# Flat weight loads of 4.5 rows per partition, one transfer for wo, w2 in halves, and 128 of its rows in three row pieces

## The chip, the cores and the metric

One core of a Trainium2 chip. The time is the device time of one execution in microseconds (us); each kernel is run several times, always beside runs of the kernel before on the same chip. "The record" of a transfer is its entry in the trace: queue, start, duration and size of each packet. The records of a load to 128 partitions are 128 packets and 16 semaphore writes, so I count 8 packets for each of the 16 DMA engines. A semaphore write is the packet by which an engine reports that its part of a load is done; the last of the 16 is the load's landing. The records do not say which engine a packet ran on.

## The reference

A decode step: attention over a window of 2,048 cached positions, and a squared-ReLU MLP beside it, for two tokens.

```python
# B, Sq, D = 2, 1, 576;  Hq, Hkv, Sk, Dh = 32, 16, 8192, 128;  F = 4608;  all bf16
xn = layernorm(x)
q  = (xn @ wq)                               # wq: 576 x 4096
k, v = last 2048 positions of the caches     # 2 x 16 x 2048 x 128 each
o  = softmax(q k^T * Dh**-0.5) v
h  = relu(xn @ w1 + b1) ** 2                 # w1: 576 x 4608
out = x + o @ wo + h @ w2 + b2               # wo: 4096 x 576, w2: 4608 x 576
```

The weights and the window are 53.6 MB. Each byte is used once per call.

## The kernel before

K and V come in sixteen loads of 2 MB, 16,384 B per partition. A weight with 576 rows is 4 rows per partition plus a remainder of 64 rows. wo comes in two transfers, w2 in four row groups, whose last is itself cut. 256 rows of w2 do not fit that scheme: they come by small loads on the scalar queue, w2x, four of 5 partitions x 8 rows each and one of 96 partitions x 1 row.

```python
XS = ((8, 20, 5), (1, 96, 96))               # (rows per partition, partitions, partitions per load)
# ... cut ...
def issue_w2x():
    if x_parts:
        s, i = x_parts.pop(0)
        xr, xp, xe = XS[s]
        rows = B_w2[FX[s]:FX[s] + xr * xp, :].rearrange("(e i r) n -> i e (r n)", e=xe, r=xr)
        tc.keep_in_program_order(nc.scalar.dma_start(out=w2x_sb[s][i:xp:xp // xe, :], in_=rows[i]))
# ... cut: issue_w2x is called behind K and V loads, one small load each ...
W2P = [(0, 0, 9), (1, 0, 9), (2, 0, 9), (3, 0, 4), (3, 4, 6), (3, 6, 7)]     # (group, first row, last row)
# ... cut: the loop over eight units of K and V ...
for u in range(2, NU):
    step(u)
    # ... cut: load_v, load_k ...
    if u == 4:
        issue_wo(0)
        for i in range(NW):
            issue_w1(i)
wo_sel(0); wo_acc(0); issue_wo(1)
for w in W2P:
    issue_w2(*w)
```

Of the kernel before, what the change touches and what calls it, by code (L numbers as in the profile page):

```python
# [16 lines left out]
def kernel(  # L17
# [38 lines left out]
    SR = NS * NC  # L56
    assert SR == 32 and NG % NT == 0

    NFULL = D // P
    REM = D - NFULL * P  # L60
    S = P // REM
    KC = NFULL + 1
    NXN = NFULL + S
    LQ = (Hq * Dh) // S
    L1 = F // S
    NG4 = 4
    QW = Hq * Dh // NG4
    QB = QW // 2
    QH = QW // Dh
    HW = F // NG4  # L70
    HB = HW // 3
    FR = HW // P
    XS = ((8, 20, 5), (1, 96, 96))
    FT = (HW - sum(r * p for r, p, _ in XS)) // P
    F3 = (NG4 - 1) * HW
    CX = [(r, FT, P) for r in range(FT)]
    FX = []
    for xr, xp, _ in XS:
        FX.append(F3 + FT * P + sum(m * n for m, n, _ in XS[:len(FX)]))
        CX += [(FX[-1] - F3 + r, xr, xp) for r in range(xr)]  # L80
    assert FX[-1] + XS[-1][0] * XS[-1][1] == F
    N3 = (NG4 - 1) * FR
    NFC = N3 + len(CX)
    RB = 32 * (NG4 - 1) + B
# [4 lines left out]
    NP = NQ // 2  # L89
    WR = 2 * NC * Dh // P  # L90
    assert Dh // WR == NC
# [3 lines left out]
    kvpool = ctx.enter_context(tc.tile_pool(name="kvpool", bufs=6))  # L95
    ktpool = ctx.enter_context(tc.tile_pool(name="ktpool", bufs=2))
    wbig = ctx.enter_context(tc.tile_pool(name="wbig", bufs=1))
    wrem = ctx.enter_context(tc.tile_pool(name="wrem", bufs=1))
    wopool = ctx.enter_context(tc.tile_pool(name="wopool", bufs=1))
# [11 lines left out]
    out2d = out.rearrange("b s d -> (b s) d")  # L111

    k_tiles, v_tiles, wq_tiles, w1_tiles, wo_tiles, w2_tiles = {}, {}, {}, {}, {}, {}
    WBW = max(Hq * Dh, F)
    WRW = max(LQ, L1)

    def unit_view(cache, u):
        tq, b = divmod(u, B)
        return cache[b, tq * TH:(tq + 1) * TH, S0:Sk, :].rearrange("h (c j) d -> c h (j d)", c=CP)

    def issue_kv(tiles, cache, u, name, parts=1):
        tl = kvpool.tile([P, UE], BF16, tag="kv", name=f"{name}_{u}")
        v = unit_view(cache, u)
        n = UE // parts
        tiles[u] = tl
        return [lambda i=i: nc.sync.dma_start(out=tl[:, i * n:(i + 1) * n], in_=v[:, :, i * n:(i + 1) * n])
                for i in range(parts)]

    def issue_w(tiles, wt, i, name, width, lrem):
        if i == 1:  # L130
            tl = wbig.tile([P, NFULL * WBW], BF16, tag="wbig", name=f"{name}_big")
            nc.sync.dma_start(out=tl[:, 0:NFULL * width],
                              in_=wt[0:NFULL * P, :].rearrange("(p r) n -> p (r n)", r=NFULL))
            for r in range(NFULL):
                tiles[r] = tl[:, r * width:(r + 1) * width]
        else:
            tl = wrem.tile([P, WRW], BF16, tag="wrem", name=f"{name}_rem")
            nc.sync.dma_start(out=tl[:, 0:lrem], in_=wt[NFULL * P:D, :].rearrange("r (s l) -> (r s) l", s=S))
            tiles[NFULL] = tl

    def issue_wq(c):
        issue_w(wq_tiles, A_wq, c, "wq", Hq * Dh, LQ)

    def issue_w1(c):
        issue_w(w1_tiles, B_w1, c, "w1", F, L1)

    def w_rows(tiles, c, col0, n, L):
        if c < NFULL:
            return tiles[c][:, col0:col0 + n], c
        sg = col0 // L  # L150
        assert (col0 + n - 1) // L == sg
        return tiles[c][:, col0 - sg * L:col0 - sg * L + n], NFULL + sg

    def issue_wo(t):
        tl = wopool.tile([P, WR, D], BF16, tag="wo_sb", name=f"wo_{t}")
        n = P * WR
        nc.sync.dma_start(out=tl[:], in_=A_wo[t * n:(t + 1) * n, :].rearrange("(p r) n -> p r n", r=WR))
        wo_tiles[t] = tl

    w2_last = []  # L160

    def issue_w2(g, r0, r1):
        nr = FR if g < NG4 - 1 else FT
        if g < NG4 - 1:
            tl = kvpool.tile([P, nr * D], BF16, tag="kv", name=f"w2_{g}")[:]
        else:
            if r0 == 0:
                w2_last.append(wbig.tile([P, nr * D], BF16, tag="wbig", name=f"w2_{g}"))
            tl = w2_last[0][:, r0 * D:r1 * D]
        rows = B_w2[g * HW:g * HW + nr * P, :].rearrange("(p r) n -> p (r n)", r=nr)  # L170
        nc.sync.dma_start(out=tl, in_=rows[:, r0 * D:r1 * D])
        w2_tiles[(g, r0)] = tl

    const.tile([P, 96], F32, name="pad_0")
    w2x_sb = [const.tile([xp, xr * D], BF16, name=f"w2x_sb_{i}") for i, (xr, xp, _) in enumerate(XS)]
    const.tile([P, 120], F32, name="pad_1")
    x_parts = [(s, i) for s, (_, xp, xe) in enumerate(XS) for i in range(xp // xe)]

    def issue_w2x():
        if x_parts:  # L180
            s, i = x_parts.pop(0)
            xr, xp, xe = XS[s]
            rows = B_w2[FX[s]:FX[s] + xr * xp, :].rearrange("(e i r) n -> i e (r n)", e=xe, r=xr)
            tc.keep_in_program_order(nc.scalar.dma_start(out=w2x_sb[s][i:xp:xp // xe, :], in_=rows[i]))

# [7 lines left out]
    for f in issue_kv(k_tiles, A_k_cache, 0, "k"):  # L193
        f()
    NW = 2
    for i in range(NW):
        issue_wq(i)
    tmp_f = work.tile([P, NS, Dh], F32, tag="o_sb", name="tmp_f")
# [21 lines left out]
    for i in range(2):  # L220
# [7 lines left out]
    tmp_x = work.tile([P, NS, Dh], F32, tag="o_sb", name="tmp_x")  # L228
    tmp_xb = tmp_x[:].bitcast(BF16).rearrange("p s d -> p (s d)")
    xn_sb = tmp_xb[0:B, 0:D]  # L230
    nc.vector.tensor_scalar(out=xn_sb, in0=x_sb, scalar1=mv[:, 0:1], scalar2=rstd[:, 0:1],
                            op0=ALU.subtract, op1=ALU.mult)
    xr_sb = tmp_xb[0:B, D:D + S * P].rearrange("p (s k) -> p s k", s=S)
    nc.vector.memset(xr_sb, 0.0)
    for sg in range(S):
        nc.vector.tensor_copy(out=xr_sb[:, sg, sg::S], in_=xn_sb[:, NFULL * P:D])

    pro_ps = psum.tile([P, NXN, B], BF16, tag="o", name="pro_ps")
    for c in range(NFULL):
        transpose(out=pro_ps[:, c, :], in_=xn_sb[:, c:NFULL * P:NFULL], identity=ident[:B, :B])  # L240
    for sg in range(S):
        transpose(out=pro_ps[:, NFULL + sg, :], in_=xr_sb[:, sg, :], identity=ident[:B, :B])
    xnT = const.tile([P, NXN, B], BF16, name="xnT")
    nc.vector.tensor_copy(out=xnT[:], in_=pro_ps[:])

    own = const.tile([P, NC], F32, name="own")
    nc.vector.tensor_reduce(out=own[:], in_=ident[:].rearrange("p (a c) -> p c a", c=NC), axis=AX.X, op=ALU.add)
    off = const.tile([P, NC], F32, name="off")
    nc.vector.tensor_scalar(out=off[:], in0=own[:], scalar1=BIG, scalar2=-BIG, op0=ALU.mult, op1=ALU.add)
    HQ = P // 2  # L250
    of_h = const.tile([P, 3 * HQ], F32, name="of_h")
    nc.gpsimd.memset(of_h[:], 0.0)
    nc.vector.tensor_copy(out=of_h[:, HQ:2 * HQ].rearrange("p (c q) -> p c q", c=NC),
                          in_=own[:].unsqueeze(2).to_broadcast([P, NC, HQ // NC]))
# [7 lines left out]
    is_h = ident[0:TH, 0:TH].unsqueeze(1).to_broadcast([TH, NJJ * 32 // TH, TH])  # L262
    out_ps = psum.tile([RM, OQ], F32, tag="out", name="out_ps")
    nc.vector.memset(out_ps[:], 0.0)

    def out_acc(lhsT, rhs_of, start=False, stop=False):
        for i in range(4):
            matmul(out_ps[32 * i:32 * i + MB, :], lhsT=lhsT, rhs=rhs_of(i * OQ, (i + 1) * OQ), start=start, stop=stop,
                   skip_group_check=True, tile_position=(0, 32 * i))

    QZ = 2 * NC
    qz = const.tile([P, NQ, B, 2, 3 * QZ], BF16, name="qz")
    nc.gpsimd.memset(qz[:], 0.0)
    q_ps = []
    for k in range(2):
        q_ps.append(psum.tile([P, QB], F32, tag=("o", "op")[k], name=f"q_ps_{k}"))
        nc.vector.memset(q_ps[k][:], 0.0)

    def q_block(c):
        for k in range(2):  # L280
            for g in range(NG4):
                rhs, xc = w_rows(wq_tiles, c, g * QW + k * QB, QB, LQ)
                matmul(q_ps[k][32 * g:32 * g + B, :], lhsT=xnT[:, xc, :], rhs=rhs,
                                 start=(c == 0), stop=(c == KC - 1), skip_group_check=True,
                                 tile_position=(0, 32 * g))
        if c == KC - 1:
            qrow = const.tile([RB, 2 * QW], BF16, tag="row", name="qrow")
            for k in range(2):
                cp = nc.scalar.copy if k else nc.vector.tensor_copy
# [268 lines left out]
    for w in W2P:  # L558
        issue_w2(*w)
# [45 lines left out]
```

## Time and profile before

| | before |
|---|---|
| time, median of 3 runs | 134.31 us (134.27 to 134.45) |
| span in the profile | 132.6 us |
| packets on the main DMA queue (q1) | 4,032 |
| packets on the scalar queue (q10) | 178 |
| last landing (last semaphore write on q1) | 129.12 us |
| last landing to end of the span | 3.5 us |

The lines that the prediction reads are shown in it. Two more views matter later. The first is the windows view (columns: stretch, length, busy time and count of PE, PEld, DVE, ACT, POOL, granted clock, DMA share, GB/s):

```profile
19.00:30.00 11.00, 8.65 (x73) 4.06 (x73) 2.73 (x7) 2.00 (x6) 0.36 (x1) 0.66 1.01 430
50.00:61.00 11.00, 8.54 (x84) 5.05 (x82) 7.02 (x17) 5.46 (x7) 0.36 (x1) 1.00 1.00 424
```

The share says how long the engines were busy, the rate what they moved. The first stretch has a full share (1.01) at 430 GB/s; the second is full too (1.00) at 424, and it is the stretch in which the kernel's 96-row load is under way (issued at 47.2 us). The second view is the DMA issues (KB, and us to landing where known) of w2's small loads:

```profile
w2x_sb<-in_B_w_dram ACTq DMA_DIRECT2D x4, 45.0 KB
w2x_sb<-in_B_w_dram ACTq DMA_DIRECT2D x1, 108.0 KB, 8.5
```

### The profile page before, as it was taken

What the parts mean: (1) busy time and instruction counts of PE and PEld (TensorE: products, weight loads), DVE (VectorE), ACT (ScalarE), POOL (GpSimd) and SP (SyncE); (2) the same over time, 40 slices, a digit from 0 to 9 for tenths busy, and PEclk for the clock granted to TensorE, in tenths of its full rate; (3) what the DMA queues carried; (4) which work ended last, traced back from release to release, by engine and by line L of the source; (5) the groups of instructions that cost most, each with busy time, mean ns of one, the idle gap of its engine ahead of it and who ended that gap; (6) DMA issues with size and microseconds to landing.
All of it is one profiled execution on the core that took longest, in us unless ns stands there. A gap on an engine that the chain in (4) does not pass through costs nothing.

```text
span 132.6 us, 2337 instructions
## 1 busy us (share of the span) xinstructions
PE 84.1 (63%) x982; PEld 52.2 (39%) x982; DVE 57.2 (43%) x156; ACT 46.7 (35%) x64; POOL 5.2 (4%) x17
## 2 busy tenths in 40 slices
PE   0069409599597669298496599697500938655941
PEld 0068303257364436164254346354300424414930
DVE  6724400525477456566377446575400043344000
ACT  5715500418874375176265255194200040000000
POOL 6000000010010010100100100100100000000000
PEclk9999955958999999999999769999985595555595
DMA  4999999999999999999999999999999999999960
GB/s 139 409 415 488 425 397 416 430 430 415 444 418 431 433 420 427 431 430 430 418 440 420 440 430 432 421 457 432 478 405 388 425 425 450 407 423 428 416 247 1
DMA packets 4219, 53.76 MB, mean 405 GB/s; under 512 B 503, under 2 KB 730, under 8 KB 1246
## 3 DMA queue, kind: packets, MB, share of 16 engines
q1 hardware_dynamic: 4032, 53.32, 94.6%
q10 hardware_dynamic: 178, 0.31, 0.6%
q8 instruction: 7, 0.11, 0.3%
q14 instruction: 2, 0.02, 0.0%
HBM read 53.62 MB, written 0.00 MB: 404 GB/s over the span
## 4 chain that ended last, share of the span: by engine, by line
DMA 62%; PE 4%; DVE 1%; ACT 1%; issue 1%; ACTq 0%
DMA v<-in_A_v_cache_dram 29%; DMA w<-in_B_w_dram 17%; DMA k<-in_A_k_cache_dram 16%; PE kT_ps L108 3%; PE o_ps L105 1%; ACT kT L325 1%; PE sc_ps L105 1%; ACT p L357 1%; DVE pT L360 1%; DVE kT L327 0%; DVE o L386 0%; PE out_ps L105 0%; ACT fin_sb L573 0%; DVE o L384 0%; PE op_ps L105 0%
## 5 line engine op out<-in xcount | busy, mean ns | idle before, releaser
L108 PE MATMUL kT_ps<-ident_f,k 128*128 128x128 f32 x256 | 40.0, 303 | 9.3 <-DMA k<-in_A_k_cache_dram 7.0
L108 PEld LDWEIGHTS kT_ps<-ident_f,k 128*128 128x128 f32 x256 | 31.5, 155 | 22.6 <-issue 11.6
L325 ACT COPY kT<-kT_ps 128x1024 bf16<-128x1024 bf16 x32 | 32.0, 1012 | 21.8 <-PE kT_ps L108 17.4
L327 DVE COPY kT<-kT_ps 128x1024 bf16<-128x1024 bf16 x32 | 21.8, 682 | 12.9 <-PE kT_ps L108 12.7
L105 PE MATMUL sc_ps<-kT,qz 128*32 128x512 bf16 x128 | 10.3, 403 | 6.4 <-DVE kT L327 5.0
L357 ACT ACTIVATE p<-sc_ps,bias 128x512 bf16<-128x512 f32 x8 | 5.5, 688 | 17.6 <-DVE gown L353 17.6
L105 PE MATMUL o_ps<-v,pT 128*32 128x512 bf16 x128 | 11.6, 461 | 0.0
L105 PEld LDWEIGHTS <-xnT 128*2 128x2 bf16 x100 | 3.1, 112 | 17.7 <-issue 17.5
L105 PE MATMUL h_ps<-w_big,xnT 128*2 128x384 bf16 x48 | 3.6, 484 | 7.9 <-DMA w_big<-in_B_w_dram 7.9
L346 DVE TENSOR_REDUCE m<-sc_ps 128x1 f32<-128x512 f32 x8 | 5.5, 692 | 7.1 <-PE sc_ps L105 7.1
L386 DVE SCALAR_TENSOR_TENSOR o<-o_ps,in_s,o 128x128 f32<-128x128 f32 x24 | 8.3, 348 | 0.5
L360 DVE STREAM_TRANSPOSE pT<-p 128x512 bf16<-128x512 bf16 x8 | 5.7, 711 | 6.5 <-ACT p L357 6.5
L573 ACT CAST fin_sb<-out_ps 113x144 bf16<-113x144 f32 x1 | 0.3, 279 | 21.8 <-PE out_ps L105 21.8
L105 PE MATMUL q_ps<-wq_big,xnT 128*2 128x512 bf16 x32 | 3.6, 625 | 5.0 <-DMA wq_big<-in_A_wq_dram 5.0
L350 POOL PARTITION_ALL_REDUCE gmax<-m x8 | 2.9, 365 | 88.8 <-DVE m L348 88.8
L384 DVE TENSOR_SCALAR o<-o_ps,in_s 128x128 f32<-128x128 f32 x8 | 2.7, 341 | 8.1 <-PE o_ps L105 8.1
L451 DVE TENSOR_TENSOR hrow<-t 98x384 bf16<-98x384 f32 x3 | 1.6, 557 | 10.6 <-ACT t L450 10.5
L105 PEld LDWEIGHTS <-qz 128*32 128x32 bf16 x128 | 2.2, 96 | 10.1 <-DVE kT L327 7.5
L105 PE MATMUL op_ps<-o,of_h 128*128 128x129 f32 x16 | 3.9, 333 | 3.2 <-DVE o L386 3.2
L105 PEld LDWEIGHTS <-hT_sb 128*17 128x17 bf16 (+2 forms) x172 | 4.3, 116 | 3.2 <-issue 3.2
L105 PE MATMUL out_ps<-w,hT_sb 128*17 128x144 bf16 x136 | 4.1, 279 | 2.1 <-DMA w<-in_B_w_dram 2.0
L450 ACT ACTIVATE t<-h_ps 98x384 f32<-98x384 f32 x3 | 1.4, 489 | 11.0 <-PE h_ps L105 10.7
(74 smaller groups left out, 52.8 us busy)
## 6 DMA issues: line engine op xcount, KB each, us to landing
k<-in_A_k_cache_dram SPq DMA_DIRECT2D x8, 2048.0 KB, 18.3
v<-in_A_v_cache_dram SPq DMA_DIRECT2D x8, 2048.0 KB, 9.9
wo<-in_A_wo_dram SPq DMA_DIRECT2D x2, 2304.0 KB, 27.2
w_big<-in_B_w_dram SPq DMA_DIRECT2D x1, 4608.0 KB
wq_big<-in_A_wq_dram SPq DMA_DIRECT2D x1, 4096.0 KB, 17.8
w<-in_B_w_dram SPq DMA_DIRECT2D x3, 1296.0 KB, 31.6
w_rem<-in_B_w_dram SPq DMA_DIRECT2D x1, 576.0 KB, 28.0
w<-in_B_w_dram SPq DMA_DIRECT2D x1, 576.0 KB, 22.1
```

The costliest lines, as they stand in the source:

```text
L105: tc.keep_in_program_order(nc.tensor.matmul(*a, **k))
L108: tc.keep_in_program_order(nc.tensor.transpose(*a, **k))
L325: nc.scalar.copy(out=kT, in_=kT_ps[:])
L327: nc.vector.tensor_copy(out=kT, in_=kT_ps[:])
L346: nc.vector.tensor_reduce(out=m1[:], in_=sc_ps[:], axis=AX.X, op=ALU.max)
L350: nc.gpsimd.partition_all_reduce(gmax[:], m2[:], channels=P, reduce_op=ReduceOp.max)
L357: nc.scalar.activation(out=p_sb[:], in_=sc_ps[:], func=ACT.Exp, bias=bias[:, 0:1], scale=scale, accum_out=o1[:, Dh:Dh + 1])
L360: nc.vector.transpose(out=pT[:].rearrange("p j r -> p (j r)"), in_=p_sb[:])
L384: nc.vector.tensor_scalar(scalar1=in_s[:, 0:1], scalar2=None, op0=ALU.mult, **kw)
L386: nc.vector.scalar_tensor_tensor(scalar=in_s[:, k:k + 1], in1=o1[:, 0:Dh], op0=ALU.mult, op1=ALU.add, **kw)
L450: nc.scalar.activation(out=t1, in_=mlp["ps"][k][0:RB, :], func=ACT.Relu)
L451: nc.vector.tensor_tensor(out=hrow[:, k * HB:(k + 1) * HB], in0=t1, in1=t1, op=ALU.mult)
```

## The change

The intent is fewer and larger packets, and small loads that are spread better over the DMA engines. wq, w1 and wo are each read flat, in one transfer, with 4.5 rows per partition. A row that straddles two partitions is handled by a stationary tile (the operand that TensorE holds while the weights stream past it) of four columns, two tokens x two halves. wo moves to the end. w2 is two halves of 18 rows per partition: the first half is one transfer, the second comes as rows 0 to 8, 9 to 13, 14 to 15 and 16 on the main queue. Its row 17, one row of 1,152 B for each of 128 partitions, is the new w2x, cut into partitions 0 to 84, 85 to 116 and 117 to 127. The change was also described as bringing K and V in 16 KB packets; that was already so. The core of the diff, cut:

```diff
-    NFULL = D // P
-    REM = D - NFULL * P
-    XS = ((8, 20, 5), (1, 96, 96))
+    W2P = [(0, 9), (9, 14), (14, 16), (16, 17)]
+    XS = [(0, 85), (85, 117), (117, 128)]
 ...
+    def issue_flat(w, name):
+        n = w.shape[0] * w.shape[1] // P
+        tl = wbig.tile([P, NH * L1], BF16, tag="wbig", name=name)
+        nc.sync.dma_start(out=tl[:, 0:n], in_=w.rearrange("r n -> (r n)").rearrange("(p l) -> p l", p=P))
+        return tl
 ...
+    for p0, p1 in XS:
+        nc.scalar.dma_start(out=w2x_sb[p0:p1, :], in_=w2_rows[1, p0:p1, (FR - 1) * D:FR * D])
     step(1)
     load_k(4)
 ...
-    wo_sel(0)
-    wo_acc(0)
-    issue_wo(1)
-    for w in W2P:
-        issue_w2(*w)
+    mlp_h(w1_sb)
+    wo_sb = issue_flat(A_wo, "wo")
 ...
+    nc.sync.dma_start(out=w2a_sb[:], in_=w2_rows[0])
+    nc.sync.dma_start(out=w2b_sb[:], in_=w2_rows[1, :, 0:r9 * D])
+    for r0, r1 in W2P[1:]:
+        nc.sync.dma_start(out=w2c_sb[:, (r0 - r9) * D:(r1 - r9) * D], in_=w2_rows[1, :, r0 * D:r1 * D])
```

## The prediction

> **What bounds the kernel now.** I read the page's 40 slices and packet counts first, because the reference reads every weight and cache byte once and does little arithmetic with it:
>
> ```profile
> PE   0069409599597669298496599697500938655941
> ...
> DMA  4999999999999999999999999999999999999960
> ...
> DMA packets 4219, 53.76 MB, mean 405 GB/s; under 512 B 503, under 2 KB 730, under 8 KB 1246
> ...
> q1 hardware_dynamic: 4032, 53.32, 94.6%
> q10 hardware_dynamic: 178, 0.31, 0.6%
> ```
>
> The DMA row is at 9 from the second slice to the last but two, while PE has holes. The reader is to see that no engine waits for long because of its own work: 94.6% + 0.6% of 132.6 us is 126.2 us of packets on each of 16 DMA engines, in a span that holds about 127 us between the first packet and the last. Next, the windows view at the two ends (columns: stretch, length, busy time and count of each engine, clock, DMA share, GB/s):
>
> ```profile
> 22.00:42.00 20.00, 16.22 (x143) 9.53 (x135) 10.56 (x26) 11.18 (x17) 0.73 (x2) 0.87 1.01 429
> ...
> 62.00:82.00 20.00, 14.72 (x132) 8.74 (x130) 12.28 (x30) 9.29 (x12) 0.73 (x2) 0.91 1.01 431
> ...
> 126.00:127.00 1.00, 0.00 (x0) 0.00 (x0) 0.00 (x0) 0.00 (x0) 0.00 (x0) 0.94 0.99 393
> 127.00:128.00 1.00, 0.74 (x36) 0.59 (x36) 0.00 (x0) 0.00 (x0) 0.00 (x0) 1.00 0.73 280
> 128.00:129.00 1.00, 0.43 (x16) 0.28 (x16) 0.00 (x0) 0.00 (x0) 0.00 (x0) 1.00 0.41 144
> 129.00:130.00 1.00, 0.59 (x12) 0.24 (x11) 0.00 (x0) 0.20 (x1) 0.00 (x0) 0.77 0.01 2
> ```
>
> In the middle the share is 1.01 at 427 to 431 GB/s: full. At the end it falls to 0.73 and 0.41 while the last bytes come: some DMA engines are done at 127.0 and others at 129.1. If all finished together they would finish about (1 - 0.73) + (1 - 0.41) + 0.1 = 0.96 us earlier. That is the only idle DMA time after the start. Third, the chain in order of time, and the timeline at the end:
>
> ```profile
> 68.31 39.02 DMA v<-in_A_v_cache_dram
> 107.33 0.02 issue
> 107.34 22.09 DMA w<-in_B_w_dram
> ```
>
> ```profile
> 128.39 0.43 PE L105 MATMUL out_ps<-w,hT_sb 128*17 128x144 bf16 x16 [0.65 <-DMA w<-in_B_w_dram]
> 129.10 0.66 PE L105 MATMUL out_ps<-w,hT_sb 128*17 128x144 bf16 x12 [0.28 <-DMA w<-in_B_w_dram]
> 129.80 0.28 ACT L573 CAST fin_sb<-out_ps 113x144 bf16<-113x144 f32 x1 [21.76 <-PE out_ps L105]
> 130.11 0.63 ACTq L574 DMA_DIRECT2D out_dram<-fin_sb  x1
> ```
>
> The chain's long pieces are issue-to-landing times in a full queue, so they are queueing, not latency. After the last byte (129.1) come four matmuls, a cast and the store: 132.6 - 129.1 = 3.5 us.
>
> **What the Trainium skill says.** "DMA: Bandwidth & Descriptors", Where 436 GB/s comes from, puts the ceiling at 435 GB/s; the 427 to 431 of the windows agree: no room in the rate. The same page, Why small descriptors are slow, names a fixed overhead per packet. The trace's packet records agree that one exists: packets of 1,152, 16,384 and 36,864 B take 51, 611 and 1,364 ns (medians), a line of 36.7 ns per 1,000 B plus 9 ns. The same page, Why a DMA increments its semaphore by 16 and not by 1, says a load uses the largest number of engines up to 16 that divides its slowest dimension, the lowest-numbered ones. The records agree in the count: each 5-partition w2x load left 5 semaphore writes and the 2-partition load of x left 2. By that, the 85-partition piece of the change goes to 5 engines, the 32-partition piece to 16, the 11-partition piece to 11.
>
> **The change part by part.** Bytes: the five tensors and both caches are read once before and after, 53.6 MB. K and V were 16 KB packets already (2,048 packets of 16,384 B in the records), so that part of the description moves nothing.
>
> *Packets, the main queue.* Per DMA engine a 128-partition load has 8 packets. Before, outside K and V: 4,096 + 32,768 (wq), 4,608 + 36,864 (w1), 2 x 18,432 (wo), 3 x 10,368, 4,608, 2,304, 1,152 (w2): 159 + 1,213 + 178 + 1,364 + 2 x 686 + 3 x 389 + 178 + 93 + 51 = 5,775 ns, x 8 = 46.20 us. After: wq and wo 36,864 each, w1 41,472 (1,364 + 4,608 x 0.0367 = 1,533), w2 20,736 (771), 10,368 (389), 5,760 (220), 2,304 (93), 1,152 (51): 5,785 ns, x 8 = 46.28 us. One more row of w2 per partition comes through here, for 12 loads turned into 8. With four semaphore writes of 9 ns fewer per engine: +0.04 us.
>
> *Packets, the scalar queue.* w2x before: four loads of 5 x 9,216 B (347 ns) and 96 rows of 51 ns. Engines 0 to 4 carry 4 x 347 + 6 x 51 = 1.69 us, the others 0.31. After, 128 rows of 51 ns: engines 0 to 4 carry 17 + 2 + 1 = 20 rows, 1.02 us; the others 2 or 3, 0.10 to 0.15. Engine 0 also carried four b1 packets of 93 ns; it now has two of about 51. So with the +0.04: engines 0 to 4 gain 0.6 us, engine 0 about 0.9, the others 0.1 to 0.2. The mean gain is some 0.29 us, which is about 31 packets fewer per engine at 9 ns.
>
> *Which engine ends last.* The last load's 16 semaphore writes in the records stand from 128.24 to 129.12, with 128.86 next to last. One engine trails by about 0.3 from 50 us on, when the 2,304 B packets of b1 have gone by; I take it for engine 0. The ones behind it can be those that served the seven 16 KB instruction fetches (queue 8; each pushes one engine back by roughly 1 us). Engine 0 comes forward by 0.9, to 128.2; the fetch engines by only 0.13, from 128.86 to 128.7. The end of the stream then moves from 129.12 to about 128.7: 0.4 us. That the fetches fall as before is assumed.
>
> *TensorE.* The q product goes from 40 matmuls of 512 columns to 36; the stationary tile has four columns for two, and a moving column costs the same. h goes from 60 of 384 to 72 of 288: at 2.40 us for 32 in the timeline at half clock (75 ns each), 4.5 us becomes 72 x 75 x 0.75 = 4.1. Output products: 64 + 64 for wo as before, w2 140 for 172 with its remainder. h's transposes go from 25 to 18. All of it lies under the stream and is worth nothing unless it delays a load.
>
> *VectorE.* The selection of wo's stationary runs for each of eight units, not twice. Before it is 0.17 + 0.18 + 0.42 + 0.59 = 1.36 us in the timeline near 120; on 32 partitions and one batch I estimate 0.9 per unit. Eight of these against two: +4.5 us on an engine 43% busy.
>
> *Moves in the queue.* wo is now one load at the end, in the buffer that w1 leaves, so it can only be issued when h's matmuls end. Work back from 128.7 at 0.43 MB/us: w2's last eight rows take 2.7 us, the nine before them 3.1, its first half 6.2, wo 11.0. So wo has to start at 105.7; v6, v7 and k7 at 4.9 each lie ahead of it, and w1 lands at 91. h is then done near 91 + 4.1 + a little = 96, ten us before the queue would run dry. After wo lands (116.7) TensorE needs 128 x 33 ns (64 took 2.10 us) = 4.2 us before w2's first half is there at 122.9; it keeps up. The last piece is again one row, four matmuls, so the tail of 3.5 us stays.
>
> Sum: 0.4 us less of stream, nothing else: 134.3 - 0.4 = 133.9 us.
>
> **The rivals.** (a) *A hole in the stream.* If h is late, wo, and with it everything to the end, is late one for one. For it: one buffer for wq, w1 and wo, and loads behind it in the same issue order. Against: ten us of slack, and the kernel before ran the same kind of hand-over:
>
> ```profile
> SPq L171 <- PE h_ps L105: 4.0, 1, 4.0
> SPq L157 <- PE out_ps L105: 3.8, 1, 3.8
> ```
>
> with no dip in the DMA row. It would cost 1 to 4 us. (b) *ScalarE held by its own small loads.* Loads share eight completion semaphores in turn, as the trace's operands show; a load waits for the one that used its semaphore last. With eight large loads issued at the top, the b1 and w2x loads on the scalar queue may wait for K and V landings up to about 39 us, and ScalarE's copies of kT behind them. Then K's buffers come free late. I count the fourth K load then being issued near 46, when the queue still has work to about 48: no loss, but close; a miss costs 1 to 3 us. (c) *Nothing gained.* If a fetch or a reload of ACT's tables lands on the trailing engine anyway, the end stays at 129.1: 134.2. (d) *All imbalance gone*: the mean gain 0.3 plus nearly 1 us: 133.1.
>
> **Range and chances.** The centre is 133.9. (c) and (d) bound the normal outcome, 133.1 to 134.3; (a) and (b) together have perhaps one chance in ten, mostly under 2% (2.7 us). I give 133.2 to 134.6 for 8 in 10. Over 2% faster would need 131.6, below what full balance of the engines gives: 0.02. Slower than 137.0 needs a hole of 3 us: 0.04. Within 2%: 0.94.
>
> **What would show it.** Right: about 576 fewer main-queue packets (32 data packets and four semaphore writes on each of 16 engines), the DMA row still 9 throughout, the middle still near 430 GB/s, the last one-row load landing at 128.4 to 129.0, a tail of 3.5 us, and the share in the last two us of the stream higher than 0.73 and 0.41. wo's issue should come near 96 with v7 landing near 105. Wrong: a slice of the DMA row below 9 between 10 and 125 us (a hole, rivals a or b), TensorE still working through wo when the last rows land, a packet of 41,472 B far from 1,533 ns, or a last landing that has not moved although engines 0 to 4 carry less.

## The result, and the profile after

| | before | after |
|---|---|---|
| time, median | 134.38 us (134.27 to 134.50) | 135.39 us (135.20 to 135.52) |
| ratio after / before, 95% interval | | 1.0074 (1.0057 to 1.0092) |
| span in the profile | 132.6 us | 133.7 us |
| packets on the main queue | 4,032 | 3,456 |
| last landing | 129.12 us | 130.04 us |
| last landing to end of the span | 3.5 us | 3.7 us |

A ratio is the mean time of one kernel's runs over that of the other's runs of the same rounds, so it is not quite the ratio of the medians. The change costs 1.0 us where I predicted a gain of 0.4. It counts as the same at 2%, but the interval is well clear of 1, and 135.39 is outside my range of 133.2 to 134.6.

The page of the changed kernel, its slices and its DMA queues:

```profile
PE   0079419599598497599779778204729971739461
...
DMA  4999989999999999999999999999999998999940
...
DMA packets 3660, 53.76 MB, mean 402 GB/s; under 512 B 439, under 2 KB 706, under 8 KB 962
...
q1 hardware_dynamic: 3456, 53.46, 94.3%
q10 hardware_dynamic: 194, 0.16, 0.4%
```

The same bytes in 576 fewer main-queue packets, as predicted. There are two 8s in the DMA row. They tell nothing: versions below that lose no time show 8s at the same place near 18 us and again after 110. What does not fit is the share. 94.3% + 0.4% of 133.7 us is 126.6 us of packets per engine, against 126.2 before. With fewer packets of the predicted sizes it should have gone down. Something made packets longer. The chain of waits (start, us, what) at its end, and the timeline there:

```profile
61.17 30.87 DMA w<-in_B_w_dram
...
92.08 4.22 PE h_ps L94 x72
...
96.31 0.34 SPq L119
...
97.64 31.76 DMA w2c<-in_B_w_dram
...
129.44 1.41 PE out_ps L94 x32
```

```profile
129.44 1.39 PE L94 MATMUL out_ps<-w2c,hT_sb 128*17 128x144 bf16 x32 [0.47 <-DMA w2c<-in_B_w_dram]
...
130.88 0.28 ACT L459 CAST fin_sb<-out_ps 113x144 bf16<-113x144 f32 x1 [18.35 <-PE out_ps L94]
```

The hand-over from w1 to wo went as planned: h's matmuls take 4.2 us from 92.1, wo is issued at 96.3, and the queue does not run dry. TensorE then waits for the last rows of w2, as before; they come later. Now the windows:

```profile
19.00:30.00 11.00, 8.74 (x70) 4.54 (x70) 2.82 (x10) 2.04 (x6) 0.36 (x1) 0.66 1.00 408
...
127.00:128.00 1.00, 0.29 (x12) 0.28 (x15) 0.00 (x0) 0.00 (x0) 0.00 (x0) 0.50 0.87 340
128.00:129.00 1.00, 0.97 (x35) 0.77 (x25) 0.00 (x0) 0.00 (x0) 0.00 (x0) 0.50 0.50 188
129.00:130.00 1.00, 0.56 (x20) 0.56 (x20) 0.00 (x0) 0.00 (x0) 0.00 (x0) 0.50 0.10 36
```

This is the loss. Between 19 and 30 us the engines are busy all the time and move 408 GB/s, where they moved 430 before: 22 GB/s short for 11 us is 0.24 MB, or 0.24 / 0.43 = 0.56 us. At the end the drain is also longer: a share of 0.10 is left after 129. The packets' records agree. In this stretch the 16,384 B packets of the main queue have a median of 635 ns, and 83% of them take over 620; before it was 611 and 10%. What else ran then? The three w2x pieces, issued at 5.4 to 6.4 us, whose rows trickle through until 30.3:

```profile
w2x_sb<-in_B_w_dram ACTq DMA_DIRECT2D x1, 95.6 KB
w2x_sb<-in_B_w_dram ACTq DMA_DIRECT2D x1, 36.0 KB
...
w2x_sb<-in_B_w_dram ACTq DMA_DIRECT2D x1, 12.4 KB
```

The 85-partition piece left 5 semaphore writes: it runs on five engines, 17 rows of 51 ns each. Five engines would carry 31% of the large packets, and 83% are long: so a load on five engines would be lengthening packets on most of the others too. One more thing stands in SyncE's waits (total us, times, longest):

```profile
SPq L106 <- DMA w2x_sb<-in_B_w_dram: 9.7, 2, 8.6
```

K and V loads share completion semaphores with the pieces, and the queue's issuing engine waits for them. That is a rival.

### The profile page after: what moved, and what is told of

Read it like the earlier page. It is cut to its first block, busy times and chain, and to the rows that moved or that the text cites.

```text
span 133.7 us, 2291 instructions
## 1 busy us (share of the span) xinstructions
PE 85.7 (64%) x949; PEld 53.5 (40%) x949; DVE 64.6 (48%) x184; ACT 46.7 (35%) x67; POOL 4.9 (4%) x15
## 2 busy tenths in 40 slices
DMA packets 3660, 53.76 MB, mean 402 GB/s; under 512 B 439, under 2 KB 706, under 8 KB 962
## 3 DMA queue, kind: packets, MB, share of 16 engines
q1 hardware_dynamic: 3456, 53.46, 94.3%
## 4 chain that ended last, share of the span: by engine, by line
DMA 77%; PE 17%; SPq 2%; DVE 1%; ACT 1%; issue 1%; ACTq 0%; DVEq 0%
DMA w2c<-in_B_w_dram 24%; DMA w<-in_B_w_dram 23%; DMA k<-in_A_k_cache_dram 16%; DMA wq<-in_A_wq_dram 14%; PE kT_ps L97 6%; PE h_ps L94 3%; PE q_ps L94 3%; PE o_ps L94 1%; PE sc_ps L94 1%; PE out_ps L94 1%; SPq L106 1%; DVE qrow L237 1%; ACT qrow L237 0%; DVE qz L253 0%; SPq L442 0%
## 5 line engine op out<-in xcount | busy, mean ns | idle before, releaser
L97 PE MATMUL kT_ps<-ident_f,k 128*128 128x128 f32 x256 | 42.3, 318 | 6.0 <-DMA k<-in_A_k_cache_dram 4.0
L97 PEld LDWEIGHTS kT_ps<-ident_f,k 128*128 128x128 f32 x256 | 34.0, 164 | 19.0 <-issue 11.5
L94 PEld LDWEIGHTS <-xnT 128*4 128x4 bf16 x108 | 3.5, 119 | 15.8 <-issue 14.2
L94 PE MATMUL h_ps<-w,xnT 128*4 128x288 bf16 x72 | 4.2, 421 | 7.0 <-DMA w<-in_B_w_dram 7.0
L94 PE MATMUL q_ps<-wq,xnT 128*4 128x512 bf16 x36 | 4.0, 627 | 4.9 <-DMA wq<-in_A_wq_dram 4.9
L375 DVE TENSOR_TENSOR hrow<-t 100x1152 bf16<-100x1152 f32 x2 | 2.6, 1355 | 8.5 <-ACT t L373 8.5
L94 PE MATMUL op_ps<-o,of_h 128*32 128x129 f32 x16 | 3.7, 316 | 4.6 <-DVE o L334 4.6
L97 PE MATMUL pro_ps<-ident,xn_sb 2*128 2x2 bf16 x5 | 0.9, 181 | 6.8 <-DVE xn_sb L172 6.5
L94 PEld LDWEIGHTS <-hT_sb 128*17 128x17 bf16 x144 | 3.4, 106 | 4.2 <-issue 4.0
L237 DVE CAST qrow<-q_ps 100x512 bf16<-100x512 f32 x1 | 0.7, 691 | 8.2 <-PE q_ps L94 8.2
```

The source lines that it names most:

```text
L94: tc.keep_in_program_order(nc.tensor.matmul(*a, **k))
L97: tc.keep_in_program_order(nc.tensor.transpose(*a, **k))
L237: cp(out=qrow[:, k * QW:(k + 1) * QW].rearrange("p (i a d) -> p i a d", a=2, d=Dh), in_=q_ps[0:RB, k * QW // 2:(k + 1) * QW // 2].rearrang ...
L375: nc.vector.tensor_tensor(out=h4[:, :, k * HB:(k + 1) * HB], in0=t4, in1=t4, op=ALU.mult)
```

## The experiments

For each kernel I add up, over all main-queue packets of a stretch, the time above the undisturbed median of that packet size (611 ns for 16,384 B, 1,364 ns for 36,864 B, and so on) and divide by 16. I call this the *extra packet time*. It is 0.11 us before and 0.63 us after, for 8 to 31 us. "Excess" is the median minus the median of the kernel before in the same set.

### First set: is it the pieces?

The theory: the pieces on the scalar queue lengthen everybody's packets. The rivals: the loss comes from the rest of the change; or from the time at which the pieces are issued. First a control, the changed kernel unaltered.

> The changed kernel unaltered, as the control of this set. In its trace the 16,384-byte packets between 19 and 30 us take 630 to 660 ns on all 16 engines, not 611 as later and as in the kernel before, and the last load's semaphore writes spread from 128.5 to 130.0 us. Both theories expect 135.3 to 135.5 us. If the slow packets or the one trailing engine (0.4 us behind the next) are an accident of one execution they will be absent here.

Measured: 135.42 us against 134.41, ratio 1.0077 (1.0064 to 1.0090). Its extra packet time is 0.69 us. The loss is stable.

One load in place of three:

```diff
-    XS = [(0, 85), (85, 117), (117, 128)]
+    XS = [(0, 128)]
```

> One 128-row w2x load in place of the pieces of 85, 32 and 11 rows, same place on the scalar queue: 8 packets of 1,152 B on each of 16 engines. Theory P (the piece on five engines makes all engines' packets longer while it trickles through): packets between 19 and 30 us return to 611 ns, all engines gain about 0.5 us, and engines 0 to 4 no longer carry 0.9 us more than the rest; 134.3 to 134.8 us. Theory S (the slow stretch comes from what else runs at the start, such as the earlier issue of the first five K and V loads): packets stay at 630 to 660 ns in that stretch and the time falls by at most 0.3, to 135.0 to 135.4.

Measured: 134.44 against 134.41, ratio 1.0001 (0.9987 to 1.0014). The loss is gone, whole, with one line. The windows of this kernel:

```profile
19.00:30.00 11.00, 8.43 (x76) 4.01 (x76) 2.98 (x11) 2.90 (x7) 0.36 (x1) 0.76 1.01 433
...
127.00:128.00 1.00, 1.00 (x37) 0.85 (x29) 0.00 (x0) 0.00 (x0) 0.00 (x0) 0.50 0.56 211
128.00:129.00 1.00, 0.90 (x29) 0.61 (x27) 0.00 (x0) 0.00 (x0) 0.00 (x0) 0.50 0.29 106
129.00:130.00 1.00, 0.62 (x15) 0.27 (x11) 0.00 (x0) 0.28 (x1) 0.00 (x0) 0.50 0.00 0
```

The same bytes, on the same queue, at the same time, and the rate is 433, not 408. Extra packet time: 0.07 us. The last landing is at 128.88, 1.16 us earlier than after. The shorter packets are about half of that (0.63 - 0.07 = 0.56 us); the rest is that the 16 engines end closer together, which is worked out further below.

The same three pieces, 50 us later:

```diff
-    for p0, p1 in XS:
-        nc.scalar.dma_start(out=w2x_sb[p0:p1, :], in_=w2_rows[1, p0:p1, (FR - 1) * D:FR * D])
     step(1)
 ...
     for u in range(2, NU - 1):
         step(u)
+        if u == 3:
+            for p0, p1 in XS:
+                tc.keep_in_program_order(nc.scalar.dma_start(out=w2x_sb[p0:p1, :], in_=w2_rows[1, p0:p1, (FR - 1) * D:FR * D]))
```

> The same three pieces of w2x, issued after the fourth step (near 55 us) instead of at 5 us. Theory P: the slow packets move with the pieces, to some 12 us after 55 us, and the stretch from 19 to 30 us is at 611 ns; total time about the same, 135.1 to 135.5. Theory S: the stretch from 19 to 30 us stays slow and none appears after 55 us; time about the same. The trace decides here, not the time.

Measured: 135.47 against 134.41, ratio 1.0078 (1.0066 to 1.0091).

```profile
19.00:30.00 11.00, 9.23 (x73) 5.04 (x73) 2.86 (x10) 2.50 (x7) 0.36 (x1) 0.66 1.01 432
...
60.00:72.00 12.00, 10.00 (x89) 5.37 (x87) 8.52 (x24) 6.62 (x8) 0.36 (x1) 1.00 1.02 410
```

The slow stretch moved with the pieces: 432 GB/s where it had been 408, and 410 in the stretch after their issue at 55 us (the changed kernel, unaltered, has 427 there). The 16,384 B packets at 60 to 72 us have a median of 642 ns, 84% over 620. The loss belongs to the pieces, not to their place.

The row through the main queue, as one 128-partition load:

```diff
-    for p0, p1 in XS:
-        nc.scalar.dma_start(...)
+    nc.sync.dma_start(out=w2x_sb[:], in_=w2_rows[1, :, (FR - 1) * D:FR * D])      # between wo and w2a
     nc.sync.dma_start(out=w2a_sb[:], in_=w2_rows[0])
 ...                                       # its product moved behind wo's products
```

> The w2x row as one 128-partition load on the main queue between wo and the first half of w2, nothing of it on the scalar queue. Theory P: like the single load or a little better, 134.2 to 134.7 us, all 16 engines equal but for the instruction fetches, and packets at 611 ns from 10 us on. Theory S: 134.9 to 135.3. A second theory of the end, F (one engine trails because late instruction fetches fall on an engine that is late already), expects the last semaphore write to be still some 1 to 1.5 us after the first ones, now set by fetches alone.

Measured: 134.39 against 134.41, ratio 0.9999 (0.9986 to 1.0011). Taking the pieces off the scalar queue gains nothing over one load there (e1). So the queue as such is not the cause.

### Second set: which pieces, and is the change needed for it?

Two theories were open: the load on five engines is what hurts (85 has no larger divisor up to 16 than 5), or having pieces of fewer than 128 rows at all. The cuts 80/32/16 and 88/32/8 put the large piece on 16 and on 11 engines, by the rule that the prediction cites. The records agree: the scalar queue has 63 and 50 semaphore writes in these two, for 47 after.

```diff
-    XS = [(0, 85), (85, 117), (117, 128)]
+    XS = [(0, 80), (80, 112), (112, 128)]     # f1
+    XS = [(0, 88), (88, 120), (120, 128)]     # f2
```

> The changed kernel with w2x cut into 80, 32 and 16 rows: the same number of small loads on the same queue at the same place, but each on 16 engines. The whole 1 us was shown to come from the cut of 85, 32 and 11. If it is the few engines of the first piece (theory E: 17 small packets each on five engines, one after every large one), packets stay at 611 ns and the time is that of the single load, 134.3 to 134.6. If it is that the rows of a piece do not fall on the same engines as those of a 128-row load (theory M), the packets between 18 and 23 us are longer by 10 to 40 ns for the five rounds that the 80 rows take, and the time is 134.5 to 134.9.

> w2x cut into 88, 32 and 8 rows, so that the first piece should go to 11 engines with 8 packets each. Theory E: fewer engines than 16 but eight rounds, so a slowing of between a fifth and a half of that of the 85 rows: 134.5 to 134.8. Theory M: as f1 or more, over eight rounds (18 to 24 us), packets longer by 10 to 40 ns, 134.6 to 135.0.

Measured: f1 134.78 against 134.35, ratio 1.0030 (1.0017 to 1.0044); f2 134.83, ratio 1.0031 (1.0016 to 1.0046). More engines, and over half of the loss stays away, but not all of it. The packets are still long: in f1 a median of 659 ns from 18 to 23.5 us and 611 after that; in f2 655 from 18 to 25. So the large piece hurts on 16 engines as well; it is only through sooner.

Next, the kernel *before*, with nothing changed but its own 96-row load cut as 85 + 11:

```diff
-            tc.keep_in_program_order(nc.scalar.dma_start(out=w2x_sb[s][i:xp:xp // xe, :], in_=rows[i]))
+            cuts = (0, 85, xp) if xe == xp else (0, xp // (xp // xe))     # two loads for the 96-row one alone
+            for e0, e1 in zip(cuts, cuts[1:]):
+                st = xp // xe
+                tc.keep_in_program_order(nc.scalar.dma_start(out=w2x_sb[s][i + st * e0:i + st * (e1 - 1) + 1:st, :],
+                                                             in_=rows[i][e0:e1]))
```

> The kernel before with one edit: its load of 96 one-row partitions is cut into 85 and 11, so that the piece on five engines is in it alone. If this piece is the cause, packets lengthen to 630 to 660 ns on all engines for some 12 us from 50 us on, and the time rises by 0.5 for that plus up to 0.55 because engines 0 to 4, late already, carry 11 more small packets of 51 ns: 135.0 to 135.5 us. If the cause needs something else of the change (the flat weights, the earlier K and V issues), it stays at 134.4 to 134.9.

Measured: 135.41 against 134.35, ratio 1.0076 (1.0063 to 1.0090).

```profile
50.00:61.00 11.00, 7.99 (x66) 4.27 (x65) 5.23 (x14) 4.72 (x6) 0.36 (x1) 0.84 1.03 418
60.00:72.00 12.00, 9.91 (x83) 6.07 (x79) 6.74 (x16) 5.00 (x8) 0.36 (x1) 0.84 1.00 421
```

The whole loss, with none of the rest of the change: a share of 1.03 and 1.00 at 418 and 421 GB/s, where the kernel before has 424 and 429. This is the strongest run. The flat weights, the four-column tiles, wo at the end and w2's halves are not needed for the loss, and e1 has them all without it.

In the same set I tried what could be gained at the end of the stream, since e1 and e3 showed nothing of my 0.4 us: e3 with the last pieces of w2 cut finer.

```diff
-    W2P = [(0, 9), (9, 14), (14, 16), (16, 17)]
+    W2P = [(0, 10), (10, 14), (14, 16), (16, 17)]     # f3
+    W2P = [(0, 12), (12, 15), (15, 16), (16, 17)]     # g3, in the third set
```

> The main-queue version of w2x with the last pieces of w2 cut as 10, 4, 2 and 1 rows instead of 9, 5, 2 and 1. In the single-load run TensorE worked without a wait from 128.24 to 129.62 through the last 8 rows, 0.7 us past the last landing. Theory T (part of the stream's gain is eaten by TensorE's last matmuls): a four-row piece lands later relative to the end but needs 16 matmuls, not 20; 0.05 to 0.2 us less than 134.39, so 134.2 to 134.35. If the tail is set by the last landing alone: 134.39 again.

> The tail version further: last pieces of w2 12, 3, 1 and 1 rows instead of 10, 4, 2 and 1. Theory T: TensorE has 20 matmuls after the 12-row piece instead of 28, and the time falls by another 0.05 to 0.1 from 134.24. If the last landing alone sets it: 134.2 to 134.3.

Measured: f3 134.24 against 134.35, ratio 0.9991 (0.9978 to 1.0003); g3 134.46 against 134.32, 1.0010 (0.9997 to 1.0024). Neither is told from 1. The cuts at the end are not where the 0.4 us went.

### Third set: the number of loads, or their rows?

g1 keeps three small loads but cuts the row by columns: each load has all 128 partitions, with 384 B each, so it makes three times as many packets. g2 has only two loads, of 64 rows each.

```diff
-    for p0, p1 in XS:
-        nc.scalar.dma_start(out=w2x_sb[p0:p1, :], ...)
+    for c in range(0, D, D // 3):             # g1
+        nc.scalar.dma_start(out=w2x_sb[:, c:c + D // 3],
+                            in_=w2_rows[1, :, (FR - 1) * D + c:(FR - 1) * D + c + D // 3])
```

```diff
-    XS = [(0, 85), (85, 117), (117, 128)]
+    XS = [(0, 64), (64, 128)]                 # g2
```

> The changed kernel with w2x again as three loads at the same place, but cut by columns: each load has all 128 partitions and 384 B of each. The 80-row cut showed that 16 engines do not save it, so theory E has fallen. Theory M (rows of a load with other than 128 partitions go over other engines than those of the large loads beside them, and this makes the large packets longer) expects 611 ns packets throughout and 134.4 to 134.6 us. Theory L (several small loads beside the large ones do it, whatever their rows) expects packets of 630 to 660 ns while they run, and 134.7 to 135.0.

> w2x cut into two loads of 64 rows, four rows on each of 16 engines in each. Theory M: longer packets, 625 to 660 ns between about 18 and 24 us, as with 80 rows; 134.6 to 134.9 us. Theory L: two loads lengthen packets too, but the column cut shows the same. If packets are at 611 here, it is not the number of partitions as such.

Measured: g1 134.30 against 134.32, ratio 0.9996 (0.9982 to 1.0010); g2 135.04, ratio 1.0054 (1.0040 to 1.0067). In g1:

```profile
19.00:30.00 11.00, 8.86 (x69) 4.32 (x69) 2.42 (x8) 2.04 (x6) 0.36 (x1) 0.66 1.02 431
```

More packets on the scalar queue and no loss: neither the number of loads nor of small packets matters. Two loads of 64 rows, which use all 16 engines evenly, lose 0.7 us. Their extra packet time is 0.70 us, and the last landing is 0.62 us later than in g1 (129.52 for 128.90). So five engines are not needed for a loss.

These two also judge the rival of SyncE's wait. g1 has such a wait and loses nothing:

```profile
SPq L106 <- DMA w2x_sb<-in_B_w_dram: 7.1, 2, 4.5
```

g2 has no line of this kind and loses 0.7 us. The wait is hidden by the queue's depth; it is not the cause.

Between the two stands a load that is a little lopsided, 96 + 32:

```diff
-    XS = [(0, 85), (85, 117), (117, 128)]
+    XS = [(0, 96), (96, 128)]                 # h1
```

> w2x cut into 96 and 32 rows, six and two on each of 16 engines. The kernel before has a 96-row load of this kind at 50 us, and there only three packets in ten were longer than 620 ns. Theory M as stated (any load of other than 128 rows) expects the stretch from 18 to 24 us to be slow as with 80 rows, 134.6 to 134.9 us; if 96 rows are harmless here too, 134.4 to 134.6 us and nearly all packets at 611 ns, M has to be narrowed to which rows meet, and the number 128 is not what matters.

Measured: 134.56 against 134.45, ratio 0.9981 (0.9910 to 1.0052). The interval is wide because two of the seven runs of the kernel before were at 135.6, so the ratio decides nothing. The records say more: in 17 to 25 us 32% of the 16,384 B packets are over 620 ns, at a median of 613: a mild form. The kernel before has the same load of 96 rows, and the same mild form (29% over 620 at 50 to 55 us). There the 96 rows lie side by side in w2; in h1 they lie 20,736 B apart.

### Fourth set: how many rows, or which?

Two theories could still explain all that: fewer rows than 128 in a load (N), or rows that lie in one half of the partitions, 0 to 63 or 64 to 127 (H). In g2 both are true. i1 takes 64 rows per load as well, but every second partition; i2 takes the middle 64 and two loads of 32, one in either half.

```diff
-    for p0, p1 in XS:
-        nc.scalar.dma_start(out=w2x_sb[p0:p1, :], in_=w2_rows[1, p0:p1, (FR - 1) * D:FR * D])
+    for s in range(2):                        # i1
+        nc.scalar.dma_start(out=w2x_sb[s:P:2, :], in_=w2_rows[1, s:P:2, (FR - 1) * D:FR * D])
```

```diff
-    XS = [(0, 85), (85, 117), (117, 128)]
+    XS = [(32, 96), (0, 32), (96, 128)]       # i2
```

> w2x in two loads of 64 rows, one of the even partitions and one of the odd ones. Theory N (a load of fewer than 128 rows slows the others, by its number of rows): packets of 640 to 660 ns between 17 and 24 us as with the first 64 rows, 134.9 to 135.1 us. Theory H (a load is slow for all when its rows lie in one half of the partitions, so that its 16 engines write into half of them): nearly all packets at 611 ns and 134.3 to 134.6 us.

> w2x in the 64 rows 32 to 95 first, then rows 0 to 31, then 96 to 127. Theory N: as slow as two loads of 64, 134.9 to 135.1 us. Theory H: the first load (four of eight rounds) is harmless, the two of 32 rows, each in one half, are not; the slow stretch is about half as long, 134.5 to 134.8 us.

Measured: i1 134.46 against 134.32, ratio 1.0009 (0.9994 to 1.0023); i2 134.50, ratio 1.0011 (0.9994 to 1.0028). The windows at 17 to 24 us of g2 and then of i1, and i2's at 19 to 30 us:

```profile
17.00:24.00 7.00, 3.85 (x36) 1.08 (x35) 0.00 (x0) 0.00 (x0) 0.00 (x0) 0.63 0.97 394
```

```profile
17.00:24.00 7.00, 4.01 (x36) 1.08 (x35) 0.23 (x1) 0.00 (x0) 0.00 (x0) 0.51 1.00 424
```

```profile
19.00:30.00 11.00, 8.69 (x69) 4.38 (x69) 2.49 (x8) 2.04 (x6) 0.37 (x1) 0.66 1.01 423
```

i1 has the same number of loads and of rows as g2 and the same packets of 1,152 B; the partitions differ, and with them the rows of w2 that are read. In 17 to 25 us its 16,384 B packets have a median of 611 ns and none is over 620; g2's have 644 and 56%. N has fallen, H stands. In i2 40% are over 620, at a median of 614.5 ns: half of its rows come by loads that lie in one half. The times of i1 and i2 are not told apart; the packets are.

One rival is not separated by g2 and i1: each partition reads its own row of w2, so another choice of partitions is also another choice of places in memory. Two pairs speak against it. The 85-row piece is slow with rows 20,736 B apart (e0) and with adjacent rows (f4), and 96 rows are mild with rows apart (h1) and adjacent (the kernel before).

### All of it in one table

| kernel | loads of the row | excess, us | extra packet time, us | 16,384 B packets: median ns, share over 620 |
|---|---|---|---|---|
| after, again (e0) | 85 / 32 / 11 | 1.01 | 0.69 | 640, 83% |
| late (e2) | 85 / 32 / 11 | 1.06 | 0.65 (60 to 80 us) | 642, 84% |
| before, 85 (f4) | 85 / 11 | 1.06 | 0.60 (50 to 70 us) | 644, 69% |
| g2 | 64 / 64 | 0.72 | 0.70 | 644, 56% |
| f2 | 88 / 32 / 8 | 0.48 | 0.82 | 655, 91% |
| f1 | 80 / 32 / 16 | 0.43 | 0.54 | 659, 84% |
| i2 | middle 64 / 32 / 32 | 0.18 | 0.22 | 614.5, 40% |
| h1 | 96 / 32 | 0.11, wide | 0.23 | 613, 32% |
| i1 | 64 even / 64 odd | 0.14 | 0.05 | 611, 0% |
| e1 | 128 | 0.03 | 0.07 | 611, 0 to 1% |
| g1 | 3 x 128, by columns | -0.02 | 0.05 | 611, 0 to 1% |

The last column is taken where the loads are under way (19 to 30 us for e0, e1 and g1, 17 to 25 for g2, h1, i1 and i2, 18 to 25 for f2, 18 to 23.5 for f1, 60 to 72 for e2, 50 to 62 for f4). Every kernel with clearly long packets is slow, none without is, and the two mild ones (i2, h1) lie close to the kernel before. The sizes agree only roughly. f2 seems to have more extra packet time than it loses (0.82 against 0.48), but its profiled run was its slowest, 135.19 us, 0.84 above the kernel before. The 85-row kernels lose 0.3 to 0.5 more than theirs. For them the end gives the rest. From the packets after 126 us one can work out the mean time at which the 16 engines end. The last landing comes 1.3 to 1.5 us after that mean in the 85-row kernels (after, e0, e2, f4) and 0.8 to 1.0 in all others, the kernel before among them. So one engine or a few trail by half a microsecond more. That fits an estimate: by the prediction's rule for the number of engines, each of five engines carries 12 rows of 51 ns more than in e1 (or, in f4, than in the kernel before), which is 0.6 us.

## Why the prediction was wrong

**The bound, the bytes, the packets: right.** The DMA engines bind, there were 576 fewer main-queue packets, and a packet of 41,472 B took 1,533 ns, as worked out; 20,736 B took 771. At their undisturbed sizes the main queue's packets add up to 0.04 us more per engine, as predicted. In all, each engine has 35 packets fewer (4,219 to 3,660 in sum), where I counted 31.

The change of the span can be split into three terms that add up. The mean end of the 16 engines is worked out from the packets after 126 us; the predicted second term is 0.4 less 0.29.

| us, against the kernel before | predicted | after | e1 (one load) |
|---|---|---|---|
| mean end of the 16 engines | -0.29 | +0.32 | -0.32 |
| last landing behind that mean (0.87 before) | -0.1 | +0.59 | +0.08 |
| last landing to end of the span (3.52 before) | 0 | +0.17 | +0.25 |
| span in the profile (sum, before rounding) | -0.4 | +1.09 | +0.01 |

**"Packets, the scalar queue": the step that failed.** I gave each small packet its 51 ns on its own engine and nothing else, so that engines 0 to 4 would gain 0.6 us and all of them 0.29 in the mean. In its place the runs showed that the rows lengthen the large packets of most engines, from 611 to 635 to 660 ns for as long as they trickle. That term was zero in my sum; it measured 0.63 us after and 0.69 in the repeat, less 0.07 in e1. The mean gain itself was sized rightly: without the pieces it came (-0.32 in e1). That the pieces do it is shown by e1 (undone, gone), e2 (moved, moves along) and f4 (put alone into the kernel before, all there). That the place of the rows can do it is shown for loads of 64 rows by g2 against i1, but for the rival of the source rows, named there. That the 85-row piece, with 64 rows in the lower half and 21 in the upper, is slow for the same reason is argued from the order of the table, not shown.

Why a row's place should matter is argued, not shown: no record names the place where two packets meet. The Trainium skill offers a reading. "SBUF — State Buffer", Door 1: The DMA port swizzle, says that a partition's number decides which of 16 ports a DMA reaches it by, and that partitions 0 to 63 reach only eight of them. "DMA: Bandwidth & Descriptors", The descriptor swizzle, says that in a 128-partition load each engine writes one port. Then a load in one half, if all 16 engines share it, must send half of them to ports that the other engines are filling, and both may wait there. The cases can be read so: 64 rows in one half are bad, 96 (both halves, unevenly) are mild, and 64 that alternate are harmless if each engine's rows stay in its own half. How the rows of such a load are dealt to engines is in no record, so it stays a reading; and it does not say why 85 rows on five engines should slow most of the sixteen.

**"Which engine ends last": wrong in size and sign.** I put the last landing at 128.7 and it was 130.04. About 0.6 us of the shift is the longer packets, which no balance of the small ones can mend. The rest is balance: I had said that moving rows off engines 0 to 4 would bring the last engine nearer to the others, and it fell further behind, by 0.59 us. The premise fails too. With nothing of w2x on the scalar queue (e3) the last landing is still 0.89 us behind the mean, as in the kernel before, so the small loads were not what held the last engine back there. One reading of mine was wrong as well: 128.24 to 129.12 are the last 16 semaphore writes of the main queue, not those of the last load. Packets of the load before it, of 2,304 B, run until 128.74, and the first of the last load's own packets begin at 126.44; the engines end over some two microseconds, not 0.9.

**The gain of 0.4: not there either.** Without the pieces the change is worth 0.03, -0.02 and -0.02 us (e1, e3, g1). In their profiles the last landing is 0.2 to 0.35 us earlier than before, but the intervals hold only gains up to about 0.2 us. In e1 and e3 the time from there to the end grew by 0.25 and 0.24 us, which takes all of it in e1 and two thirds in e3. In e1 TensorE begins its last 32 matmuls at 128.24, before the last row has landed, and takes until 129.62 at a granted clock of 0.50; but in e3 the clock is 1.00 there and the end is as late. In g1 the end did not grow, and its profiled run was 0.2 us shorter than that of the kernel before. Why the rest does not show in the medians is open.

**"Moves in the queue", TensorE, rivals (a) and (b): right.** h's matmuls took 4.2 us (4.1 predicted), w1 landed at 92.0 (91), wo was issued at 96.3 (96), the tail was 3.7 us (3.5), and all stayed under the stream. A q matmul of 512 moving columns took 627 ns with four stationary columns and 625 with two. ScalarE's loads were issued together at 4 to 6.4 us and nothing of rival (b) was seen; the load of k4, the fifth of K, went out at 33.8. **VectorE: undersized, without effect.** The selection took 1.07 us per unit, not 0.9, so it added 5.9 us, not 4.5, all off the path. The rival that I did not have is the one that came: a transfer that slows other transfers. My own check, "the middle still near 430 GB/s", would have caught it, and did: 408.

## What to carry to other kernels

When transfers bind, read DMA share and GB/s side by side: a full share at a lower rate means that the same bytes take longer. Look then whether packets of one size have become longer, and for what else runs in that stretch. Give even a tiny side load all 128 partitions, cut by columns if it must be cut (g1), or at least alternate partitions (i1): 144 KB in pieces of 85, 32 and 11 rows cost 1.0 us of a 134 us kernel, and one load of 128 rows cost nothing. Small loads are not accounted for by their own packets alone.

## What the Trainium skill lacked or had wrong

- "SBUF — State Buffer", Door 1: The DMA port swizzle, warns that a load on 64 partitions is itself slow. It gives no figure for how far such a load slows others (elsewhere the page allows that DMA engines contend on these ports): 2 x 64 rows of 1,152 B raised the 16,384 B packets of another queue from a median of 611 to 644 ns and cost 0.7 us (g2); with alternate partitions they stayed at 611 (i1).
- "DMA: Bandwidth & Descriptors", Rules for kernel authors, advises one 128-partition transfer over two in disjoint halves, since the two serialize. Here it was right for a further reason, and worth 0.7 us (excess 0.72 in g2, 0.03 with one load in e1). That two loads of alternate partitions are harmless (i1) is on no page that I read.
- The same page, Why a DMA increments its semaphore by 16 and not by 1, gives the rule for the number of engines (85 partitions left 5 semaphore writes, as it says), but not that cutting 128 rows as 85 + 32 + 11 instead of 80 + 32 + 16 costs 0.6 us more (1.01 against 0.43 of excess), with the last landing 1.34 us behind the mean end of the engines against 0.82 (e0, f1).
- The same page, Why small descriptors are slow, names a fixed overhead per packet in cycles. The records show about 9 ns per packet, and the line through 1,152 to 36,864 B also gave 41,472 B to the nanosecond (1,533).
